# Two gated layers behind an attention: a Silu gate, sums off TensorE, products in pieces, new step tables

## The chip, the cores and the metric

The kernel runs on one core of a Trainium2 chip. The metric is the device time of one execution in microseconds; less is better. The core's engines are named as in the profile: PE is TensorE (PEld its weight loads), DVE is VectorE, ACT is ScalarE, POOL is GpSimd, SP is the engine whose queue issues the DMAs.

## The reference

```python
# q, k, v: (8, 8, 576, 64); phi: (8, 8, 576, 32)
a = exp(phi - max(phi, axis=2)); a = a / (sum(a, axis=2) + 1e-9)
k_m = einsum('bhsm,bhsd->bhmd', a, k)
v_m = einsum('bhsm,bhsd->bhmd', a, v)
scores = 1 / sqrt(64) * q @ k_m.T
attn = exp(scores - max(scores)); attn = attn / (sum(attn) + 1e-9)
x = (attn @ v_m) as (4608, 512)          # tokens x (heads * 64)
h = x @ w_in;  g = h / (1 + exp(-1.702 * h));  x = g @ w_out      # first layer, d_ff 2048
h = x @ w_in2; g = h / (1 + exp(-h));          out = g @ w_out2   # second layer
```

## The kernel before

The whole program is one list of instructions per engine, written in an order that tables set; each engine takes its own in order. Every product is made in three passes over high and low halves of the operands (PASSES), so that a tile of the first layer's hidden values is six matmuls.

**First stage: attention and the first layer's first product.** The outer loop runs over 128 steps, 16 for each of the 8 batches: two halves `i` of a batch's tokens (288 each) by eight blocks `f` of 256 hidden columns. A step has three slots, `x = 3 * s + u`. Slots u = 0 and 1 call `first`, which makes one h tile (128 hidden columns by 288 tokens, six matmuls into one of four banks of PSUM) and gates it; slot u = 2 stores the pair of gated tiles to DRAM (`store`). Before a slot's `first`, everything that the tables put on that slot is emitted. The gate was Tanh on ScalarE (L390) and a combining step on VectorE (L391) that reads the bank once more; the result is twice g, and the factor 0.25 in `b_copy` and `b_add` (with the product's own structure) takes it back.

The first product's weights depend on the batch: w' = v_m @ w_in, made in four blocks of 512 columns, `wp_mm` (TensorE, L340), `wp_hi` and `wp_lo` (high and low half of a slab). So each batch needs, ahead of its first h tile: loads of phi, k, v, q; the maximum of phi (`phi_max` and three small steps); `phi_sub`, `phi_exp`; `kv_mm`, 9 chunks of eight products of key and value with the exponentials, 144 matmuls (L207); the sums of the exponentials; `kv_norm`, `kv_t`, `kv_e`; six transposes of q (`q_t`, `q_e`); and for each half `scores`, `soft1`, `soft_sub`, `soft_exp`, `soft2`, `soft_mul`, `soft3`, `soft_hi`, `soft_lo`. Batches 2 to 7 take the sums on GpSimd (`phi_sum`, five adds) and one small product (`es_mm`); batches 0 and 1 take them on TensorE, by matmuls of two columns inside `kv_mm` (L214, 144 in each batch).

`TIMES` gives for batches 1, 2, 3 and all later ones the slot of every step, relative to the batch's first slot 48b; `on` says which of two engines does some of them. `FIRST` is the order of everything ahead of slot 0 (batch 0, and the weight tiles 0 to 3 that make column block 0 of w_in), and `BEGIN` places the rest of w_in's 16 tiles and batch 0's last steps. A weight tile is loaded (`w1_load`, L59, 0.5 MB), then converted by two steps on ScalarE (L78, L88), one on VectorE (L96) and one on GpSimd (L98). `WO` places the same for the first layer's w_out.

All DMAs are issued by SP in program order. Four banks of PSUM serve all of the attention's small products (`psa`), four the h tiles.

**Later stages.** From 382 us on the first layer's second product (`middle`, L787), then the second layer (L571, L686). They read what the first stage stored.

## Time and profile before

| | |
|---|---|
| median of 3 runs | 1441.04 us (1438.67 to 1444.81) |
| profiled execution | 1444.52 us, its span 1442.5 us |
| busy share of the span | PE 96%, PEld 92%, DVE 72%, ACT 55%, POOL 22% |
| mean granted TensorE clock | 0.989 |
| DMA | 277 MB, mean 192 GB/s |

Times in the rows are microseconds from the start of the span. Busy time is the time in which an engine had an instruction running; matmuls overlap each other, so that a busy TensorE is not one at its peak. "Idle before" names how long the engine stood still ahead of an instruction, and what released it.

### The profile page before, as it was taken

What the parts mean: (1) busy time and instruction counts of PE and PEld (TensorE: products, weight loads), DVE (VectorE), ACT (ScalarE), POOL (GpSimd) and SP (SyncE); (2) the same over time, 40 slices, a digit from 0 to 9 for tenths busy, and PEclk for the clock granted to TensorE, in tenths of its full rate; (3) what the DMA queues carried; (4) which work ended last, traced back from release to release, by engine and by line L of the source; (5) the groups of instructions that cost most, each with busy time, mean ns of one, the idle gap of its engine ahead of it and who ended that gap; (6) DMA issues with size and microseconds to landing.
All of it is one profiled execution on the core that took longest, in us unless ns stands there. A gap on an engine that the chain in (4) does not pass through costs nothing.

```text
span 1442.5 us, 26633 instructions
## 1 busy us (share of the span) xinstructions
PE 1385.5 (96%) x10288; PEld 1324.9 (92%) x10288; DVE 1044.5 (72%) x1490; ACT 794.4 (55%) x1395; POOL 323.9 (22%) x225
## 2 busy tenths in 40 slices
...
GB/s 343 191 172 262 262 286 267 267 270 186 328 282 165 263 92 225 214 135 236 87 122 191 199 174 196 215 154 218 167 194 186 208 89 132 202 49 187 125 106 33
DMA packets 217727, 276.99 MB, mean 192 GB/s; under 512 B 50689, under 2 KB 198145, under 8 KB 217601
## 3 DMA queue, kind: packets, MB, share of 16 engines
...
q8 instruction: 80, 1.31, 0.4%
q14 instruction: 47, 0.38, 0.1%
...
## 4 chain that ended last, share of the span: by engine, by line
PE 87%; DMA 3%; ACT 2%; DVE 2%; issue 2%; SPq 0%; POOL 0%; DVEq 0%; ACTq 0%; POOLq 0%
PE p L686 24%; PE pb L787 24%; PE xb L571 14%; PE h L388 10%; PE y L571 10%; PE a L340 2%; DMA g1s<-g 1%; DMA w1t<-wq 1%; PE a L207 1%; PE a L253 1%; ACT g L390 1%; DMA rawe<-in_moe_w_out_dram 1%; PE a L276 1%; DVE g L391 1%; DMA phi<-in_phi_dram 0%
## 5 line engine op out<-in xcount | busy, mean ns | idle before, releaser
L787 PE MATMUL pb<-op,wq 128*128 128x384 f32 x2016 | 350.5, 335 | 1.3 <-ACT op L766 0.8
L787 PEld LDWEIGHTS pb<-op,wq 128*128 128x128 f32 x2016 | 349.7, 188 | 1.9 <-ACT op L766 1.1
L686 PE MATMUL p<-op,wq 128*128 128x384 f32 x2016 | 351.0, 335 | 0.0
L686 PEld LDWEIGHTS p<-op,wq 128*128 128x128 f32 x2016 | 349.6, 188 | 1.3 <-DVE op L462 1.3
L462 DVE TENSOR_TENSOR op<-rr,op 128x768 fp32r<-128x768 f32 x204 | 238.0, 1176 | 49.1 <-ACT op L671 26.6
L388 PEld LDWEIGHTS h<-attnT,slab 128*128 128x128 f32 x1536 | 213.8, 193 | 37.5 <-DVE g L391 14.5
L388 PE MATMUL h<-attnT,slab 128*128 128x288 f32 x1536 | 237.2, 307 | 9.2 <-DVE g L391 3.8
L571 PE MATMUL xb<-xq,wq 128*128 128x384 f32 x1152 | 216.8, 337 | 0.3 <-ACT e L620 0.2
L571 PEld LDWEIGHTS xb<-xq,wq 128*128 128x128 f32 x1152 | 201.4, 188 | 1.4 <-ACT e L620 0.5
L866 POOL TENSOR_TENSOR c<-c 128x512 int32<-128x512 int32 x32 | 49.7, 1553 | 614.4 <-DVE c L864 526.8
L462 DVE TENSOR_TENSOR op<-r,op 128x768 fp32r<-128x768 f32 x132 | 144.9, 1106 | 37.8 <-ACT op L766 25.1
L391 DVE SCALAR_TENSOR_TENSOR g<-g,h 128x288 f32<-128x288 f32 x256 | 108.6, 447 | 84.3 <-ACT g L390 83.8
L571 PE MATMUL y<-xq,wq 128*128 128x384 f32 x864 | 166.2, 336 | 0.2 <-ACT e L631 0.2
L571 PEld LDWEIGHTS y<-xq,wq 128*128 128x128 f32 x864 | 151.6, 188 | 0.5 <-ACT e L631 0.5
L390 ACT ACTIVATE g<-h 128x288 f32<-128x288 f32 x256 | 100.3, 415 | 92.1 <-PE h L388 77.3
L671 ACT CAST op<-rr 128x768 fp32r<-128x768 f32 x108 | 89.7, 838 | 98.5 <-PE p L686 63.1
L580 ACT ACTIVATE gq<-e 128x384 f32<-128x384 f32 x144 | 75.6, 525 | 102.7 <-DVE e L459 101.6
L766 ACT CAST op<-rr 128x768 fp32r<-128x768 f32 x96 | 79.9, 835 | 68.0 <-PE pb L787 39.9
L459 DVE TENSOR_TENSOR e<-e,y 128x384 f32<-128x384 f32 x96 | 52.8, 553 | 60.8 <-PE y L571 53.7
L766 ACT CAST op<-r 128x768 fp32r<-128x768 f32 x72 | 60.2, 836 | 50.7 <-PE pb L787 43.6
L459 POOL TENSOR_TENSOR r<-r 128x768 f32<-128x768 f32 x10 | 22.6, 2284 | 273.5 <-DMA r<-gs 154.8
L459 DVE TENSOR_TENSOR e<-e,xb 128x384 f32<-128x384 f32 x48 | 26.5, 552 | 78.6 <-ACT c L859 34.4
...
## 6 DMA issues: line engine op xcount, KB each, us to landing
g1s<-g SPq DMA_DIRECT2D x128, 288.0 KB, 4.4
gs<-gq SPq DMA_DIRECT2D x192, 192.0 KB, 1.9
...
```

The source lines that it names most:

```text
L388: nc.tensor.matmul(out=h, lhsT=w[:, wi, g, f0:f0 + 128], rhs=x[:, xi, g * HS:(g + 1) * HS], start=(g == 0 and n == 0), stop=(g == 1 and n ...
L390: nc.scalar.activation(out=t[:, u], in_=h, func=ACTF.Tanh, scale=0.851)
L391: nc.vector.scalar_tensor_tensor(out=t[:, u], in0=t[:, u], scalar=1.0, in1=h, op0=ALU.add, op1=ALU.mult)
L459: eng.tensor_tensor(out=out, in0=a, in1=b, op=ALU.add)
L462: eng.tensor_tensor(out=out, in0=a, in1=b, op=ALU.subtract)
L571: nc.tensor.matmul(out=out, lhsT=w[:, s, wi, f0:f0 + 128], rhs=x[:, s, xi], start=(start and s == 0 and k == 0), stop=(s == 1 and k == 2), ...
L580: nc.scalar.activation(out=t, in_=h, func=ACTF.Silu, scale=2.0)
L671: nc.scalar.copy(out=t[:, :, 0], in_=s)
L686: nc.tensor.matmul(out=out[:, d], lhsT=w[:, u, wi, d * 128:(d + 1) * 128], rhs=t[:, u, gi], start=(start and p == 0 and u == 0 and k == 0) ...
L766: nc.scalar.copy(out=t[:, :, 0], in_=s)
L787: nc.tensor.matmul(out=out[:, d, :HB], lhsT=w[:, u, wi, d * 128:(d + 1) * 128], rhs=t[:, u, gi], start=(start and p == 0 and u == 0 and n ...
L866: nc.gpsimd.tensor_tensor(out=i, in0=i, in1=low, op=ALU.add)
```

## The change

The first layer's gate becomes one Silu on ScalarE with scale 1.702, which gives 1.702 g; `HALF` = 0.5 / 1.702 takes the place of 0.25 behind the second product. The sums of batches 0 and 1 are taken like those of the others, batch 0's adds on VectorE. The copies `q_e`, `soft_hi` and `wp_hi` can be on either ScalarE or VectorE, by new entries of `on` and of the tables. All of `TIMES`, `FIRST`, `BEGIN` and `WO` is new: among it the slots of the products' pieces (`k`), of the Exp steps (`exp`, and the fourth entry in each tuple of `s`) and the order of the first loads.

```diff
@@ -32,6 +32,7 @@
     NP = NF // 2
     NG = 2 * HS // 32
     scale = 1.0 / float(D) ** 0.5
+    HALF = 0.5 / 1.702
...
@@ -184,14 +185,14 @@
         t = st["phi", b][:, :, c0:c1]
         nc.scalar.activation(out=t, in_=t, func=ACTF.Exp)
 
-    def phi_sum(b):
+    def phi_sum(b, eng):
         e = st["es", b] = att.tile([128, 2, 4, M], F32, tag="kvb", name="es", bufs=2)
         t = st["phi", b]
         c = t.rearrange("p j c m -> p c j m")
         for n in range(3):
-            nc.gpsimd.tensor_tensor(out=e, in0=e if n else c[:, 0:2], in1=c[:, 2 * n + 2:2 * n + 4], op=ALU.add)
-        nc.gpsimd.tensor_tensor(out=e[:, 0], in0=e[:, 0], in1=e[:, 1], op=ALU.add)
-        nc.gpsimd.tensor_tensor(out=e[:, 0], in0=e[:, 0], in1=t[:, :, 8], op=ALU.add)
+            eng.tensor_tensor(out=e, in0=e if n else c[:, 0:2], in1=c[:, 2 * n + 2:2 * n + 4], op=ALU.add)
+        eng.tensor_tensor(out=e[:, 0], in0=e[:, 0], in1=e[:, 1], op=ALU.add)
+        eng.tensor_tensor(out=e[:, 0], in0=e[:, 0], in1=t[:, :, 8], op=ALU.add)
...
@@ -207,13 +208,6 @@
                     nc.tensor.matmul(out=a[s][32 * j:32 * j + 32, 0:2 * D], lhsT=e[p, j, c, :],
                                      rhs=t[p, :, j, (c - c0) * D:(c - c0 + 1) * D],
                                      start=(c == 0), stop=(c == C9 - 1), skip_group_check=True)
-            if b < 2:
-                for j in range(4):
-                    for s in range(2):
-                        p = slice(64 * s, 64 * s + 64)
-                        nc.tensor.matmul(out=a[s][32 * j:32 * j + 32, 2 * D:2 * D + 2], lhsT=e[p, j, c, :],
-                                         rhs=ones[p].to_broadcast([64, 2]), start=False, stop=(c == C9 - 1),
-                                         skip_group_check=True)
 
     def es_mm(b):
         es = st.pop(("es", b))[:, 0].rearrange("p j m -> p (j m)")
...
-    def q_e(b, n):
+    def q_e(b, n, copy):
         if n % 3 == 0:
             st["qT", b, n // 3] = att.tile([128, C9, 128], F32, tag="qT", name="qT", bufs=2)
         t = st["qT", b, n // 3]
         a = st.pop(("qp", b, n))[:, 0:384].rearrange("p (k x) -> p k x", k=3)
-        nc.scalar.copy(out=t[:, 3 * (n % 3):3 * (n % 3) + 3], in_=a)
+        copy(out=t[:, 3 * (n % 3):3 * (n % 3) + 3], in_=a)
...
-    def soft_hi(b, hf):
+    def soft_hi(b, hf, copy):
         t = attnT[b, hf] = moe.tile([128, 2, 2 * HS], F32R, tag="attnT", name="attnT", bufs=2)
-        nc.scalar.copy(out=tokens(t[:, 0]), in_=blocks(st["at", b, hf]))
+        copy(out=tokens(t[:, 0]), in_=blocks(st["at", b, hf]))
...
-    def wp_hi(b, c):
+    def wp_hi(b, c, copy):
         t = slab[b, c] = slabs.tile([128, 2, 2, 512], F32R, tag="slab", name="slab", bufs=4)
         for s, a in enumerate(st["wp", b, c]):
-            nc.scalar.copy(out=t[:, 0, s], in_=a)
+            copy(out=t[:, 0, s], in_=a)
...
@@ -387,8 +381,7 @@
             for n, (wi, xi) in enumerate(PASSES):
                 nc.tensor.matmul(out=h, lhsT=w[:, wi, g, f0:f0 + 128], rhs=x[:, xi, g * HS:(g + 1) * HS],
                                  start=(g == 0 and n == 0), stop=(g == 1 and n == 2))
-        nc.scalar.activation(out=t[:, u], in_=h, func=ACTF.Tanh, scale=0.851)
-        nc.vector.scalar_tensor_tensor(out=t[:, u], in0=t[:, u], scalar=1.0, in1=h, op0=ALU.add, op1=ALU.mult)
+        nc.scalar.activation(out=t[:, u], in_=h, func=ACTF.Silu, scale=1.702)
...
     def b_copy(bank):
         t = eb_tile()
-        nc.scalar.activation(out=t, in_=bank[:, :, :HB], func=ACTF.Copy, scale=0.25)
+        nc.scalar.activation(out=t, in_=bank[:, :, :HB], func=ACTF.Copy, scale=HALF)
         return t
 
     def b_add(t, bank):
-        nc.vector.scalar_tensor_tensor(out=t, in0=bank[:, :, :HB], scalar=0.25, in1=t, op0=ALU.mult, op1=ALU.add)
+        nc.vector.scalar_tensor_tensor(out=t, in0=bank[:, :, :HB], scalar=HALF, in1=t, op0=ALU.mult, op1=ALU.add)
 
...
             put(z + t["exp"][g], phi_exp, b, g)
         for n in range(4):
             put(z + t["k"][n], kv_mm, b, n)
-        if b > 1:
-            put(z + t["es"][0], phi_sum, b)
-            put(z + t["es"][1], es_mm, b)
+        put(z + t["es"][0], phi_sum, b, nc.gpsimd)
+        put(z + t["es"][1], es_mm, b)
         for x, fn in zip(t["kvt"], (kv_norm, kv_t, kv_e)):
             put(z + x, fn, b)
         for n in range(6):
             put(z + t["q"][n], q_t, b, n)
-            put(z + t["qe"][n], q_e, b, n)
+            put(z + t["qe"][n], q_e, b, n, COPY[t["on"][3][n]])
         steps = scores, soft1, soft_sub, soft_exp, soft2, soft_mul, soft3, soft_hi, soft_lo
         for hf in range(2):
             on = iter(t["on"][hf])
             for x, fn in zip(t["s"][hf], steps):
-                put(z + x, fn, b, hf, *((ENG[next(on)],) if fn in (soft_sub, soft_mul, soft_lo) else ()))
+                by = ENG if fn in (soft_sub, soft_mul, soft_lo) else COPY if fn == soft_hi else None
+                put(z + x, fn, b, hf, *((by[next(on)],) if by else ()))
         for c in range(4):
-            plan_wprime(b, c, z, t["wp"][c])
-
-    def plan_wprime(b, c, z, x):
-        for y, fn in zip(x, (wp_mm, wp_hi, wp_lo)):
-            put(z + y, fn, b, c)
+            for x, fn, a in zip(t["wp"][c], (wp_mm, wp_hi, wp_lo), ((), (COPY[t["on"][2][c]],), ())):
+                put(z + x, fn, b, c, *a)
 
     ENG = nc.vector, nc.gpsimd
+    COPY = nc.scalar.copy, nc.vector.tensor_copy
+    BY = dict(ps=ENG, ss=ENG, sm=ENG, lo=ENG, hi=COPY, qe=COPY, wh=COPY)
     TIMES = {
-        1: dict(ql=(-36, -28), max=(-39, -39, -39, -38, -38), t=(-36, -36, -34), sub=(-33, -32), exp=(-27, -26),
-                k=(-22, -18, -18, -18), es=(-20, -7), kvt=(-18, -16, -15), q=(-26, -25, -22, -20, -18, -15),
-                qe=(-22, -21, -21, -18, -17, -15),
-                s=((-13, -12, -12, -10, -9, -8, -7, -6, -6), (-6, -6, 0, 1, 1, 5, 10, 15, 22)),
-                wp=((-11, -9, -9), (-4, -2, -2), (-1, 0, 4), (3, 5, 7)), on=((1, 1, 1), (1, 0, 1))),
-        2: dict(load=(-79, -68, -57), ql=(-48, -34), max=(-74, -70, -70, -68, -67), t=(-62, -58, -56),
-                sub=(-56, -53), exp=(-54, -48), k=(-39, -39, -39, -39), es=(-44, -36), kvt=(-36, -34, -32),
-                q=(-38, -37, -35, -30, -30, -27), qe=(-37, -36, -33, -28, -27, -27),
-                s=((-25, -24, -21, -20, -19, -16, -16, -7, -3), (-8, -6, -3, 0, 2, 2, 11, 18, 20)),
-                wp=((-18, -15, -12), (-11, -9, -9), (-6, -3, 1), (6, 7, 9)), on=((1, 0, 1), (1, 1, 1))),
-        3: dict(load=(-103, -91, -82), ql=(-77, -52), max=(-97, -97, -97, -90, -89), t=(-87, -86, -83),
-                sub=(-79, -76), exp=(-74, -71), k=(-55, -55, -55, -55), es=(-56, -54), kvt=(-53, -43, -42),
-                q=(-45, -39, -38, -35, -34, -31), qe=(-40, -39, -33, -34, -34, -31),
-                s=((-30, -30, -25, -23, -20, -19, -13, -13, -9), (-14, -12, -10, -5, 1, 8, 13, 14, 16)),
-                wp=((-20, -19, -19), (-10, -4, -1), (1, 3, 3), (4, 5, 7)), on=((1, 0, 1), (0, 0, 1))),
-        4: dict(load=(-102, -96, -72), ql=(-72, -49), max=(-96, -94, -93, -89, -89), t=(-86, -82, -79),
-                sub=(-79, -79), exp=(-74, -72), k=(-55, -55, -55, -55), es=(-61, -52), kvt=(-49, -40, -38),
-                q=(-42, -41, -40, -39, -34, -32), qe=(-41, -40, -39, -34, -33, -31),
-                s=((-28, -27, -22, -20, -18, -15, -14, -12, -8), (-15, -12, -11, -7, -4, -2, 2, 9, 15)),
-                wp=((-16, -16, -16), (-13, -12, -12), (-3, 3, 3), (3, 3, 5)), on=((1, 1, 1), (1, 1, 1))),
+        1: dict(ql=(-39, -32), max=(-43, -39, -39, -38, -38), t=(-37, -36, -34), sub=(-31, -28), exp=(-28, -28),
+                k=(-23, -19, -19, -19), es=(-28, -18), kvt=(-18, -16, -15), q=(-25, -25, -22, -18, -17, -15),
+                qe=(-22, -21, -21, -18, -15, -14),
+                s=((-13, -12, -12, -10, -9, -7, -7, -5, -4), (-4, -2, 1, 2, 2, 4, 7, 9, 20)),
+                wp=((-11, -9, -9), (-1, 0, 1), (-2, -1, 3), (2, 4, 6)),
+                on=((1, 1, 0, 1), (1, 1, 0, 0), (0, 1, 0, 0), (0, 1, 0, 1, 1, 1))),
+        2: dict(load=(-74, -63, -60), ql=(-46, -37), max=(-68, -66, -66, -64, -63), t=(-58, -58, -56),
+                sub=(-56, -51), exp=(-45, -46), k=(-39, -39, -39, -39), es=(-38, -36), kvt=(-35, -34, -31),
+                q=(-37, -36, -36, -30, -29, -29), qe=(-36, -34, -34, -30, -27, -27),
+                s=((-26, -24, -22, -22, -17, -15, -15, -12, -8), (-8, -5, -3, -1, 2, 2, 3, 16, 20)),
+                wp=((-17, -17, -15), (-11, -9, -9), (-11, -7, 0), (5, 5, 9)),
+                on=((1, 1, 1, 1), (0, 0, 1, 0), (1, 1, 0, 0), (0, 1, 0, 0, 0, 1))),
+        3: dict(load=(-105, -92, -81), ql=(-83, -53), max=(-97, -97, -97, -94, -90), t=(-87, -85, -82),
+                sub=(-76, -82), exp=(-70, -70), k=(-56, -56, -55, -55), es=(-60, -54), kvt=(-52, -44, -44),
+                q=(-46, -40, -39, -37, -34, -31), qe=(-40, -38, -32, -34, -33, -31),
+                s=((-31, -31, -31, -25, -19, -19, -15, -15, -12), (-22, -10, -7, 3, 10, 15, 18, 20, 21)),
+                wp=((-20, -20, -19), (-12, -4, 2), (2, 3, 6), (5, 9, 10)),
+                on=((1, 1, 0, 0), (0, 1, 1, 1), (0, 0, 1, 1), (1, 0, 1, 0, 1, 1))),
+        4: dict(load=(-103, -98, -70), ql=(-82, -54), max=(-95, -94, -93, -91, -89), t=(-86, -82, -79),
+                sub=(-76, -74), exp=(-73, -73), k=(-56, -55, -55, -52), es=(-59, -52), kvt=(-52, -44, -40),
+                q=(-42, -41, -40, -37, -34, -32), qe=(-42, -41, -37, -35, -34, -32),
+                s=((-29, -28, -24, -24, -22, -20, -12, -7, -4), (-15, -12, -11, -7, -4, 1, 5, 8, 18)),
+                wp=((-20, -18, -14), (-13, -12, -12), (-1, 2, 3), (3, 3, 5)),
+                on=((0, 1, 1, 0), (0, 1, 0, 0), (1, 1, 1, 0), (1, 0, 1, 1, 1, 0))),
     }
...
-        fns = dict(pm=phi_max, t=phi_max_t, r=phi_max_r, b=phi_max_b, sub=phi_sub, exp=phi_exp, kv=kv_mm, lphi=load_phi,
...
         for n, (f, *x) in enumerate(FIRST):
-            if f in ("ss", "sm", "lo"):
-                x[-1] = ENG[x[-1]]
+            if f in BY:
+                x[-1] = BY[f][x[-1]]
...
     FIRST = [
-        ('lphi', 0), ('pm', 0, 0), ('lq', 0, 0), ('lkv', 0, 0), ('lkv', 0, 1), ('pm', 0, 1), ('lw', 3), ('lw', 0),
-        ('lq', 0, 1), ('lkv', 1, 1), ('pm', 0, 2), ('pm', 0, 3), ('pm', 0, 4), ('lw', 1), ('lw', 6), ('lw', 2),
-        ('t', 0), ('lw', 4), ('lkv', 1, 0), ('lw', 7), ('r', 0), ('b', 0), ('sub', 0, 0), ('sub', 0, 1),
-        ('exp', 0, 0), ('exp', 0, 1), ('lw', 5), ('kv', 0, 0), ('kv', 0, 1), ('kv', 0, 2), ('w0', 0), ('kv', 0, 3),
-        ('nrm', 0), ('qt', 0, 0), ('qt', 0, 1), ('qe', 0, 0), ('kt', 0), ('qt', 0, 2), ('qe', 0, 1), ('ke', 0),
-        ('qt', 0, 3), ('w1', 0), ('qe', 0, 2), ('qt', 0, 4), ('qe', 0, 3), ('qe', 0, 4), ('qt', 0, 5), ('lw', 8),
-        ('qe', 0, 5), ('sc', 0, 0), ('w0', 1), ('s1', 0, 0), ('w0', 3), ('ss', 0, 0, 0), ('w0', 2), ('w1', 3),
-        ('lphi', 1), ('w1', 1), ('w1', 2), ('se', 0, 0), ('wp', 0, 0), ('wh', 0, 0), ('s2', 0, 0), ('sm', 0, 0, 0),
-        ('sc', 0, 1), ('s3', 0, 0), ('hi', 0, 0), ('lo', 0, 0, 1), ('s1', 0, 1), ('wl', 0, 0), ('ss', 0, 1, 1),
-        ('se', 0, 1), ('s2', 0, 1), ('sm', 0, 1, 1),
+        ('lphi', 0), ('pm', 0, 0), ('lq', 0, 0), ('lw', 0), ('lkv', 0, 0), ('pm', 0, 1), ('lw', 1), ('lkv', 0, 1),
+        ('pm', 0, 2), ('pm', 0, 3), ('lq', 0, 1), ('lw', 2), ('pm', 0, 4), ('lw', 3), ('lw', 4), ('t', 0), ('lw', 6),
+        ('r', 0), ('lw', 7), ('b', 0), ('sub', 0, 1), ('lkv', 1, 0), ('lw', 5), ('exp', 0, 1), ('sub', 0, 0),
+        ('qt', 0, 0), ('lkv', 1, 1), ('w0', 0), ('exp', 0, 0), ('kv', 0, 0), ('qt', 0, 1), ('w1', 0), ('kv', 0, 1),
+        ('ps', 0, 0), ('kv', 0, 2), ('kv', 0, 3), ('w0', 1), ('qe', 0, 0, 0), ('w0', 2), ('es', 0), ('nrm', 0),
+        ('qt', 0, 3), ('qt', 0, 4), ('qe', 0, 3, 1), ('qe', 0, 4, 0), ('qt', 0, 5), ('w0', 3), ('kt', 0), ('w1', 1),
+        ('qe', 0, 1, 0), ('w1', 2), ('qe', 0, 5, 0), ('qt', 0, 2), ('qe', 0, 2, 1), ('ke', 0), ('w1', 3),
+        ('sc', 0, 0), ('lw', 8), ('lphi', 1), ('s1', 0, 0), ('ss', 0, 0, 1), ('se', 0, 0), ('s2', 0, 0),
+        ('sm', 0, 0, 0), ('s3', 0, 0), ('sc', 0, 1), ('hi', 0, 0, 0), ('wp', 0, 0), ('s1', 0, 1), ('lo', 0, 0, 0),
+        ('wh', 0, 0, 0), ('ss', 0, 1, 1), ('se', 0, 1), ('s2', 0, 1), ('sm', 0, 1, 1), ('wl', 0, 0),
     ]
     BEGIN = [
...
+        (15, ('w1', 8)), (5, ('lw', 12)), (13, ('w0', 12)), (5, ('w0', 5)), (20, ('lw', 15)), (16, ('lw', 14)),
+        (11, ('wp', 0, 1)), (0, ('w0', 7)), (9, ('w1', 6)), (36, ('wl', 0, 3)), (0, ('lw', 10)),
+        (33, ('wh', 0, 3, 0)), (26, ('w0', 15)), (4, ('lw', 11)), (8, ('w1', 5)), (21, ('w0', 13)), (12, ('w1', 10)),
+        (7, ('w0', 6)), (3, ('w1', 7)), (28, ('w1', 15)), (12, ('w0', 9)), (22, ('w1', 12)), (11, ('lw', 13)),
+        (3, ('lo', 0, 1, 0)), (16, ('w1', 9)), (11, ('wh', 0, 1, 0)), (11, ('wl', 0, 1)), (21, ('wp', 0, 2)),
+        (0, ('w0', 8)), (32, ('wp', 0, 3)), (2, ('hi', 0, 1, 0)), (30, ('w1', 14)), (3, ('w0', 4)), (0, ('lw', 9)),
+        (24, ('wl', 0, 2)), (21, ('wh', 0, 2, 0)), (7, ('w0', 10)), (25, ('w0', 14)), (13, ('w0', 11)),
+        (23, ('w1', 13)), (4, ('w1', 4)), (0, ('s3', 0, 1)), (16, ('w1', 11)),
...
-    WO = dict(conv=((6, 17, 19, 22), (9, 24, 26, 29), (25, 35, 38, 39), (30, 41, 42, 45)),
-              sum=((45, 47, 59), (59, 62, 70), (62, 67, 68), (54, 55, 65), (48, 58, 60, 62), (47, 67, 68, 71), (78, 78, 81, 82)))
+    WO = dict(conv=((7, 15, 16, 17), (11, 24, 26, 31), (22, 32, 39, 39), (28, 38, 39, 40)),
+              sum=((43, 46, 55), (50, 59, 63), (66, 68, 73), (58, 62, 72), (46, 55, 55, 59), (48, 67, 67, 71), (71, 78, 78, 85)))
```

## Rows read from the trace of the kernel before

**Rows 1.** Busy time by stretch: time, busy (instructions) of each engine, granted clock, DMA

```profile
0.00:100.00 100.00, 68.06 (x1033) 50.58 (x1039) 57.17 (x113) 47.88 (x95) 30.32 (x28) 0.86 0.68 232
100.00:340.00 240.00, 225.92 (x2915) 190.51 (x2904) 180.55 (x406) 163.71 (x367) 127.77 (x112) 0.99 0.80 263
340.00:388.00 48.00, 43.13 (x326) 38.44 (x325) 29.34 (x62) 27.13 (x62) 17.78 (x14) 1.00 0.78 270
388.00:1442.50 1054.50, 1048.41 (x6023) 1045.35 (x6023) 777.43 (x911) 555.70 (x874) 148.00 (x72) 1.00 0.52 168
```

**Rows 2.** Timeline of TensorE around three stalls: start, length, instructions, idle before them

```profile
67.87 1.84 PE L388 MATMUL h<-attnT,slab 128*128 128x288 f32 x12
...
82.08 0.59 PE L253 MATMUL a<-ident,q 128*128 128x128 f32 x2 [5.51 <-issue]
82.32 3.23 PE L388 MATMUL h<-attnT,slab 128*128 128x288 f32 x12
85.48 1.79 PE L340 MATMUL a<-w,kvT 64*32 64x512 f32 x16
...
91.44 1.09 PE L340 MATMUL a<-w,kvT 64*32 64x512 f32 x16
...
263.28 2.03 PE L207 MATMUL a<-kv,phi 64*32 64x128 f32 x128
267.38 0.45 PE L207 MATMUL a<-kv,phi 64*32 64x128 f32 x16 [2.07 <-issue]
...
310.16 0.41 PE L207 MATMUL a<-kv,phi 64*32 64x128 f32 x4 [2.31 <-issue]
```

**Rows 3.** The page: engines; instruction queue (packets, MB, share); one group of the second layer

```profile
PE 1385.5 (96%) x10288; PEld 1324.9 (92%) x10288; DVE 1044.5 (72%) x1490; ACT 794.4 (55%) x1395; POOL 323.9 (22%) x225
...
q8 instruction: 80, 1.31, 0.4%
...
L580 ACT ACTIVATE gq<-e 128x384 f32<-128x384 f32 x144 | 75.6, 525 | 102.7 <-DVE e L459 101.6
```

**Rows 4.** Busy time by stretch, up to two stalls and behind one, columns as above

```profile
0.00:76.65 76.65, 50.54 (x853) 38.20 (x854) 44.76 (x84) 38.59 (x76) 26.72 (x25) 0.87 0.77 269
82.10:85.50 3.40, 3.40 (x18) 3.12 (x17) 0.46 (x1) 0.78 (x2) 0.00 (x0) 0.50 0.02 5
0.00:265.60 265.60, 224.37 (x3135) 181.13 (x3135) 187.77 (x400) 161.01 (x347) 117.62 (x106) 0.95 0.78 259
```

**Rows 5.** Groups of ScalarE and VectorE, 0 to 380 us: busy, mean ns | idle before

```profile
L390 ACT ACTIVATE g<-h 128x288 f32<-128x288 f32 x252 | 98.8, 415 | 87.3 <-PE h L388 77.3 <-DMA g1s<-g 7.5 <-DMA w1t<-wq 1.8
...
L297 ACT ACTIVATE nat<-nat 128x576 f32<-128x576 f32 x16 | 11.0, 688 | 5.9 <-POOL nat L293 5.9
...
L185 ACT ACT_TABLE_LOAD x1 | 1.3, 1283 | 4.9 <-DMA phi<-in_phi_dram 4.9
...
L391 DVE SCALAR_TENSOR_TENSOR g<-g,h 128x288 f32<-128x288 f32 x252 | 107.0, 447 | 80.2 <-ACT g L390 79.7
```

**Rows 6.** Timeline of ScalarE around its second table load

```profile
386.11 1.57 ACT L766 CAST op<-rr 128x768 fp32r<-128x768 f32 x2
387.70 1.28 ACT L1075 ACT_TABLE_LOAD   x1
388.99 0.20 ACT L1075 ACTIVATE spare<-ones 128x1 f32<-128x1 f32 x1
```

**Rows 7.** Timeline of ScalarE and TensorE, batch 0 up to slot 12

```profile
16.06 0.66 ACT L78 ACTIVATE w<-rawe 128x512 f32<-128x512 f32 x1 [5.39 <-DMA rawe<-in_moe_w_in_dram]
...
30.62 2.32 PE L340 MATMUL a<-w,kvT 64*32 64x512 f32 x8 [5.18 <-POOL w L98]
...
37.86 5.44 PE L388 MATMUL h<-attnT,slab 128*128 128x288 f32 x23 [1.19 <-POOL attnT L332]
...
46.16 4.77 PE L388 MATMUL h<-attnT,slab 128*128 128x288 f32 x23 [1.40 <-POOL attnT L332]
...
53.40 1.06 PE L340 MATMUL a<-w,kvT 64*32 64x512 f32 x8 [0.38 <-POOL w L98]
...
56.00 1.78 PE L388 MATMUL h<-attnT,slab 128*128 128x288 f32 x10 [0.34 <-DVE slab L351]
```

5 lines of the change are left out of this document (3 added, 2 removed), and 8 rows, old and new, of the table BEGIN.

## The prediction

> **What bounds the kernel now.** I read busy time by stretch first, then TensorE's own timeline wherever it stood still, then the groups by line. The stretches [rows 1] say where anything can be won: after 388 us TensorE is idle for 6 us in 1054, and the diff leaves that part alone but for one constant in b_copy and b_add, so the whole question lies in the first 388 us. Up to 100 us it is idle for 32 of 100 us, and its mean granted clock is 0.86. From 100 to 340 us it is idle for 14 of 240. No other engine is full there (VectorE 181, ScalarE 164, GpSimd 128 of 240), so the stage is TensorE's plus stalls.
>
> The stalls with a name are in [rows 2]. The longest have no releaser at all, only "issue": 5.51 us right behind batch 1's key/value products, 2.07 in batch 6's, 2.31 in batch 7's. I read these as TensorE running out of instructions. Its 10288 matmuls and as many weight loads came in 80 instruction packets [rows 3], 128.6 pairs each. Up to the first two stalls 853 and 3135 matmuls are recorded [rows 4], 2282 apart or 17.8 packets (some records are missing). So I place each at a packet border, after a burst of small matmuls: 128 pairs went by in 2.03 us before the second [rows 2], where a tile of six h matmuls takes 0.92 us (12 in 1.84). Behind the long stall, in which TensorE did nothing, the granted clock is 0.50 from 82.1 to 85.5 us [rows 4], the lower level of 1.2 GHz, and 12 h matmuls take 3.23 us [rows 2].
>
> **The change part by part.**
>
> *Two-column matmuls of batches 0 and 1.* They are 144 of the 288 matmuls in a batch's burst. Without them batch 1's burst is 144 pairs, little over one packet, and the new table cuts it in 48 at slot 25 and 96 at slot 29 with three h tiles between; the loads of batch 2's keys move from slots 28 and 39 to 33 and 36, away from it. Gain: the stall, 5.51; the slow clock behind it, 3.23 - 1.84 = 1.39 for the h tiles, 1.79 - 1.09 = 0.7 for 16 products of w' (85.48 against 91.44); and the 144 pairs, at 2.03/128 = 16 ns each at most 2.3, at least 0, I take 1.5 because they interleave with wider ones. Together 9.1, bounds 2 (the stall stays, only the pairs go) and 10. What they cost instead: five adds per batch off the path (batch 0's on VectorE while TensorE still waits for k and v, batch 1's on GpSimd, which is idle 112 of 240 us) and four small matmuls, 0.1 us.
>
> *Key/value products in pieces.* Batches 4 to 7 get 48 pairs, an h tile, 64 pairs, two h tiles, 32 pairs. The packet that ran dry lasted 2.03 us and its successor came 2.07 us later, so a fetch took about 4.1 us. In the new order the first 112 pairs and three tiles, 130 pairs, last 112 x 16 ns + 3 x 0.92 = 4.6 us. That covers the fetch. Gain 2.07 + 2.31, plus a slow clock after the first like that above, about 1.4: 5.8 at most. But some 560 instructions fewer ahead shift every packet border, and batches 2 (one burst of 144) and 3 (80 and 64 with one tile between) could now hit one, for up to 2.1 us each. I take 4, bounds 0 and 5.8.
>
> *First loads and batch 0.* In the new order the second half of k and v ends 4.58 MB into the queue, where in the old one the first weight tile that was converted ended (4.59 MB, in at 16.06 us [rows 7]). So batch 0's products end near 17.5. Weight tiles 2 and 3, at the mean rate until then (0.286 MB/us), are in at about 20 and 21.7; with ScalarE, VectorE and GpSimd each taking its part of the conversion, I get w' of column block 0 started near 27, where it waited until 30.62 for GpSimd. Against that stands one thing that gets later: the low half of that block (wl) is now the last step of FIRST on VectorE, behind the other half's transposes, soft_lo and sums. The first tile's third matmul needs it, and I place it at 38.4, an estimate from walking each engine's order in FIRST; the old one went on at 37.86. Then the second half's attention is ready when the first four tiles are done, near 44.1 instead of 46.16, because soft_lo is on VectorE without waiting on GpSimd's queue, and block 1 of w' can start near 49 instead of 53.40, since VectorE has no gate steps between the shifts that GpSimd waits for. Slot 12 then starts near 52 instead of 56.00 [rows 7]. Batch 1's k and v now stand on SP's queue behind seven weight tiles; its first product is at slot 25, and 16 h tiles hide that. Gain 4, bounds -2 (the late low half and a weight that lands late each cost 3) and 8.
>
> *Gate as one Silu.* VectorE loses 256 steps of 447 ns, 114 us [rows 5], and takes back 28 copies of q, 7 of the attention's high halves and 34 of w', at L390's rate (415 ns for 288 elements) at most 0.83 us each, 57 us, and 13 of soft_lo and 8 more of soft_sub from GpSimd. VectorE, ScalarE and GpSimd all end with slack, and TensorE waits for none of them by their sum. Silu itself is no dearer than Tanh: 525 ns for 384 elements [rows 3] is 394 for 288. The h bank comes free one step sooner. I price the removed step at nothing directly, because four banks covered it.
>
> *Tables.* This is the cost. The whole first stage has one table load, ahead of the first Exp (L185); Tanh needed none [rows 5], Silu did (L1075) [rows 6]. With Silu between, every visit to Exp needs a load there and one back. Counting the Exp steps by slot, adjacent ones merged, I find 15 visits: slot 20 with both phi steps; 50, 74, 119, 167, 215 and 263 with three Exp steps; eight with one. So 30 more loads of 1.283 us, 38.5 us of ScalarE. If Silu's set held Exp as well they would fall away; no row shows it, and that is the lower bound, 0. In the trace the load stands flush: the step before it ends at 387.68, it runs from 387.70, the next starts at 388.99. A visit of one Exp blocks the gates for 2 x 1.28 + 0.69 = 3.25 us, and with the last gate before (0.42) and the first after (0.41) a bank is late by 4.1; four tiles last 3.7, and other work of TensorE between them 1.5 more (240 us held some 180 tiles of 0.92, the rest is 0.37 per tile). So a single visit is hidden, and would cost 0.4 without that cover. A triple visit, with two phi steps as long as the soft one, takes 4.6 us and is late by 5.4 against 5.2, or 3.7 uncovered: 0.2 to 1.7. Sum 1.2 to 14.5, slot 20 included. Visits come on top of w' copies queued behind, so I take 3.
>
> By the Trainium skill (ScalarE: Activation LUTs, What ACT_TABLE_LOAD costs) a switch costs 1283 ns of load and about 1380 ns of drain, 2.66 us together. The trace agrees on the load and shows no drain beside it; by the page, the triple visit would be 2.75 us longer, the sum of all visits near 33 us, and the kernel slower.
>
> *The other waits.* Of the 14 us idle from 100 to 340, 9.7 are short waits for VectorE, ScalarE and GpSimd. Fewer VectorE steps shorten some, new tables make others: 2 gained, between -3 and 6. The last 48 us (5 us idle, gates waiting for stores while the first layer's output is read back) keep the same transfers: 0. The new WO slots are hidden as they were by GpSimd's slack.
>
> Sum: 9 + 4 + 4 + 2 - 3 = 16 us.
>
> **Rivals.** *Packets still run dry* (chance 0.17): the borders move onto batches 2 and 3, and batch 1's second piece hits one while its neighbours load. For it: with the same burst batches 6 and 7 ran dry and 2 to 5 did not, so it is the border's place that decides. Against: shorter bursts. The gain of 13 falls to 3, and the time is 10 us above the forecast, 1435.
> *Table visits exposed* (0.11, ends slower): ScalarE waits in its order for an Exp whose input is late, gates behind it, and each visit shows both loads in full: 15 x 2.57 = 38.5. The sum without visits is 19, so the time is 19.5 above now, 1460. It decides from (19 + 7)/15 = 1.7 us per visit. Against it: the four banks and the 0.37 us per tile. The page's drain, named above, would bring 1441 - 19 + 33 = 1455; the chance of this rival is small because the one switch amid work shows no gap.
> *No switches needed, or more waits gone* (0.10): visits 0 and waits 6, 1441 - 9 - 8 - 6 - 6 (batch 0, pieces and waits at their bounds) = 1412.
> *Batch 0's gain is lost* (0.08): the low half of w' is later than I place it; +6, 1431.
>
> **How the numbers follow.** The profiled execution took 1444.5 us, its span 1442.5, the median is 1441.04; I take the 16 from the median: 1425. Its own range, by the terms' nearer bounds, is 1416 to 1433, chance 0.54. To hold 8 in 10 the range goes up to the packets' rival and the start of no change, 1443, and down to 1409. A measurement of this kernel can tell about 0.5%, 7.2 us. Faster 0.76 (0.54 + 0.10 + 0.08 and a quarter of the packets' rival), same 0.13 (the rest of that), slower 0.11.
>
> **What the after profile would show.** Right: no "issue" wait over 1 us inside the key/value products, granted clock 1.0 from 75 us on, wp of block 3 (slot 32) near 72 us instead of 85.48, 32 table loads in all, ScalarE 160 to 170 us busy from 100 to 340 and VectorE near 150, the end of the first stage some 16 us earlier. Wrong: TensorE waits for the gate by more than 1 us at Exp visits; h waits for the slab's low half beyond 40 us; "issue" waits at other bursts.

## The result: 1427.68 us, 1.0% faster

The median falls from 1441.65 us (1438.67 to 1444.81, 4 runs) to 1427.68 us (1424.47 to 1428.38, 4 runs), a ratio of 0.9898 with a 95% interval of 0.9872 to 0.9925. The forecast was 1425. The profiled execution took 1428.18 us, its span 1426.4; against before's 1444.52 that is 16.3 us less, where the sum said 16. So the profiles, which the points below compare, differ by some 2 us more than the medians.

The page of after, its engines and instruction queue (to be held against [rows 3]):

```profile
PE 1381.7 (97%) x10008; PEld 1318.3 (92%) x10008; DVE 1011.7 (71%) x1326; ACT 800.6 (56%) x1356; POOL 303.4 (21%) x212
...
q8 instruction: 78, 1.28, 0.4%
```

Its busy time by stretch, columns as in [rows 1]; the first stage's end is taken 14 us earlier:

```profile
0.00:100.00 100.00, 73.72 (x980) 53.52 (x981) 62.56 (x116) 62.96 (x114) 39.31 (x40) 0.95 0.82 277
100.00:340.00 240.00, 232.19 (x2823) 192.92 (x2823) 165.26 (x293) 167.92 (x336) 117.20 (x99) 1.00 0.79 257
340.00:374.00 34.00, 29.36 (x200) 28.08 (x199) 8.49 (x10) 15.87 (x38) 2.44 (x2) 1.00 0.95 310
374.00:1426.40 1052.40, 1046.46 (x6012) 1043.83 (x6010) 775.38 (x909) 553.90 (x870) 144.44 (x72) 1.00 0.52 168
```

Behind the first stage nothing moved: from the next stage's first matmul to the end it is 1061.0 us against 1060.7. Up to 100 us TensorE is busy for 73.7 instead of 68.1 us, and from 100 to 340 it is idle for 7.8 instead of 14.1.

TensorE's timeline (to be held against [rows 2] and [rows 7]): batch 0 up to slot 12, slot 32, the longest of the waits that are left (two of the four for the gate), and the next stage's first matmul:

```profile
37.27 5.20 PE L382 MATMUL h<-attnT,slab 128*128 128x288 f32 x23 [2.97 <-DVE slab L345]
42.98 3.33 PE L382 MATMUL h<-attnT,slab 128*128 128x288 f32 x23 [0.52 <-DVE attnT L326]
...
48.34 1.06 PE L334 MATMUL a<-w,kvT 64*32 64x512 f32 x8 [0.70 <-POOL w L99]
...
50.80 1.79 PE L382 MATMUL h<-attnT,slab 128*128 128x288 f32 x10 [0.19 <-DVE slab L345]
...
70.68 1.09 PE L334 MATMUL a<-w,kvT 64*32 64x512 f32 x16
...
91.32 1.68 PE L334 MATMUL a<-w,kvT 64*32 64x512 f32 x16 [1.51 <-DVE slab L345]
...
96.32 2.20 PE L208 MATMUL a<-kv,phi 64*32 64x128 f32 x138
99.98 0.42 PE L208 MATMUL a<-kv,phi 64*32 64x128 f32 x6 [1.47 <-issue]
...
119.98 2.65 PE L382 MATMUL h<-attnT,slab 128*128 128x288 f32 x18 [0.96 <-ACT g L384]
...
241.68 1.86 PE L382 MATMUL h<-attnT,slab 128*128 128x288 f32 x12 [1.10 <-ACT g L384]
...
365.44 4.40 PE L780 MATMUL pb<-op,wq 128*128 128x384 f32 x24
```

Three sums can be read off. Slot 12 starts at 50.80 instead of 56.00: 5.2 us. From there to the product of batch 0's last column block (slot 32) it is 19.88 us instead of 29.48 (85.48 - 56.00): 9.6. From there to the next stage's first matmul, 294.76 instead of 296.35 (that matmul began at 381.83): 1.6. Together 16.4.

Batches 0 and 1 go through their products without a stall; batch 2, whose burst of 144 is whole, now has one. At four of the six triple table visits TensorE waits for the gate, 0.95 to 1.10 us each. ScalarE's timeline at the visit of slot 74, the one in front of that wait:

```profile
114.65 0.41 ACT L384 ACTIVATE g<-h 128x288 f32<-128x288 f32 x1 [0.34 <-PE h L382]
115.08 1.28 ACT L291 ACT_TABLE_LOAD   x1
116.37 0.69 ACT L291 ACTIVATE nat<-nat 128x576 f32<-128x576 f32 x1
116.97 1.24 ACT L186 ACTIVATE phi<-phi 128x640 f32<-128x640 f32 x2
118.22 1.28 ACT L384 ACT_TABLE_LOAD   x1
119.52 1.32 ACT L384 ACTIVATE g<-h 128x288 f32<-128x288 f32 x4
```

From the last gate's end to the next gate's start it is 4.46 us, and the loads stand flush between their neighbours. The Trainium skill (ScalarE: Activation LUTs, What ACT_TABLE_LOAD costs) gives 1283 ns of load, which these rows show, and about 1380 ns of drain beside it, which they don't.

### The profile page after: what moved, and what is told of

Read it like the earlier page. It is cut to its first block, busy times and chain, and to the rows that moved or that the text cites. A ratio compares the mean times of both kernels' runs of the same rounds, so it can differ in the third digit from the quotient of the medians.

```text
span 1426.4 us, 25738 instructions
## 1 busy us (share of the span) xinstructions
PE 1381.7 (97%) x10008; PEld 1318.3 (92%) x10008; DVE 1011.7 (71%) x1326; ACT 800.6 (56%) x1356; POOL 303.4 (21%) x212
## 4 chain that ended last, share of the span: by engine, by line
PE 87%; DVE 3%; ACT 3%; DMA 2%; issue 2%; SPq 0%; POOL 0%; DVEq 0%; ACTq 0%; POOLq 0%
PE pb L780 24%; PE p L679 21%; PE xb L564 14%; PE h L382 11%; PE y L564 10%; PE a L334 2%; PE a L208 1%; DVE op L455 1%; PE a L247 1%; DMA g1s<-g 1%; PE a L270 1%; ACT g L384 1%; ACT L384 0%; DMA rr<-gs 0%; DMA rawe<-in_moe_w_out_dram 0%
## 5 line engine op out<-in xcount | busy, mean ns | idle before, releaser
L382 PEld LDWEIGHTS h<-attnT,slab 128*128 128x128 f32 x1536 | 210.4, 190 | 51.7 <-ACT g L384 21.3
L859 POOL TENSOR_TENSOR c<-c 128x512 int32<-128x512 int32 x32 | 46.6, 1457 | 619.2 <-DVE c L857 528.0
L759 ACT CAST op<-r 128x768 fp32r<-128x768 f32 x72 | 60.2, 836 | 52.6 <-PE pb L780 43.7
L664 ACT CAST op<-r 128x768 fp32r<-128x768 f32 x60 | 50.2, 837 | 56.5 <-PE p L679 45.1
```

The lines of the kernel that those rows point to most:

```text
L382: nc.tensor.matmul(out=h, lhsT=w[:, wi, g, f0:f0 + 128], rhs=x[:, xi, g * HS:(g + 1) * HS], start=(g == 0 and n == 0), stop=(g == 1 and n ...
L664: nc.scalar.copy(out=t[:, :, 0], in_=s)
L759: nc.scalar.copy(out=t[:, :, 0], in_=s)
L859: nc.gpsimd.tensor_tensor(out=i, in0=i, in1=low, op=ALU.add)
```

## The experiments

Each is timed against the kernel before on the same chip; ratios are to that kernel, with 95% intervals.

### Where do the stalls without a releaser come from?

The theory is that TensorE's instructions arrive in packets and that it runs dry where a packet lies whole in a burst of small matmuls. If so, useless instructions far ahead move the stalls.

**64 useless pairs in the kernel before.** At slot 6 TensorE does 32 tiny products (64 matmuls and weight loads in the trace) into a free bank; nothing else changes.

```diff
+    def idle_pairs(n):
+        h = ps_h.tile([128, 512], F32, tag="h", name="h")
+        for k in range(n // 2):
+            nc.tensor.matmul(out=h[0:32, 0:2], lhsT=ident[0:64, 0:32], rhs=ident[0:64, 0:2], start=True, stop=True)
...
-        (13, ('w1', 9)), (32, ('wp', 0, 3)), (15, ('w0', 12)), (21, ('wh', 0, 2)), (28, ('lw', 15)), (8, ('w1', 5)),
+        (6, ('idle', 64)), (13, ('w1', 9)), (32, ('wp', 0, 3)), (15, ('w0', 12)), (21, ('wh', 0, 2)), (28, ('lw', 15)), (8, ('w1', 5)),
```

> The kernel before plus 64 useless two-column matmul pairs on TensorE at slot 6, where it waits for batch 0's second attention half anyway. They compute nothing that is used. Theory of the prediction: every packet border falls 64 pairs earlier in the work behind; in batches 6 and 7 no packet lies whole in a burst any more, so the stalls of 2.07 and 2.31 us and the slow clock behind the first vanish, that of batch 1 (a burst of 192 pairs) stays. 4 to 6 us faster, ratio 0.996 to 0.997. Rival (the stalls come from the loads that run beside these bursts, or from the bursts themselves): stalls stay, the time is 0 to 1 us longer, ratio 1.000.

Measured 1434.03 us (1429.55 to 1435.42), ratio 0.9942 (0.9926 to 0.9958): added work makes the kernel 8 us faster (its profiled execution was its fastest, and shows more). That is above the 4 to 6 us expected, because batch 1's stall, which was to stay, nearly went too. Its TensorE timeline shows the added pairs, batch 1's stall cut to 0.39, and batch 7's burst whole (batch 6's is too; batch 0's stall, ahead of the added pairs, stays at 3.12; one wait of 0.81 on issue is new, behind batch 3's burst):

```profile
43.25 2.25 PE L960 MATMUL h<-ident 64*32 64x2 f32 x64 [0.72 <-DVE g L391]
...
75.47 0.34 PE L207 MATMUL a<-kv,phi 64*32 64x128 f32 x7 [0.39 <-issue]
...
293.58 2.25 PE L207 MATMUL a<-kv,phi 64*32 64x128 f32 x144
```

**126 useless pairs**, nearly one packet: the borders should fall back to where they were. The diff is to the kernel with 64.

```diff
-        (6, ('idle', 64)), (13, ('w1', 9)), (32, ('wp', 0, 3)), (15, ('w0', 12)), (21, ('wh', 0, 2)), (28, ('lw', 15)), (8, ('w1', 5)),
+        (6, ('idle', 126)), (13, ('w1', 9)), (32, ('wp', 0, 3)), (15, ('w0', 12)), (21, ('wh', 0, 2)), (28, ('lw', 15)), (8, ('w1', 5)),
```

> The kernel before plus 126 useless two-column pairs at slot 6, in place of the 64 of the earlier run: almost one whole packet (126.75 pairs by the gaps between the stalls). Theory (packet borders): every border lies again within a pair of where it was in the work, so the stalls behind batch 1 and in batches 6 and 7 are back, 1.5 to 2.5 us each in 6 and 7, 2 to 6 in batch 1; the time is that of the kernel before or up to 2 us more, ratio 0.999 to 1.002. Rival (the 64 pairs helped by keeping TensorE busy, by another bank order or by something else early on): faster as with 64 pairs, ratio 0.994.

Measured 1446.45 us (1442.02 to 1448.72), ratio 1.0037 (1.0022 to 1.0051). The stalls are back, 4.08 us behind batch 1's burst, and in batches 6 and 7 at nearly the matmuls where they were:

```profile
83.24 3.01 PE L388 MATMUL h<-attnT,slab 128*128 128x288 f32 x11 [4.08 <-issue]
...
263.71 2.15 PE L207 MATMUL a<-kv,phi 64*32 64x128 f32 x130
266.89 0.45 PE L207 MATMUL a<-kv,phi 64*32 64x128 f32 x14 [1.03 <-issue]
...
308.00 0.38 PE L207 MATMUL a<-kv,phi 64*32 64x128 f32 x2 [2.11 <-issue]
```

That tells packets from any rule of how long TensorE had been idle or busy: the two kernels differ in 62 tiny pairs at 43 us, and the stalls at 266 and 308 us come and go with them. Before has a fourth such stall, which the prediction did not read, inside batch 0's burst:

```profile
18.16 0.21 PE L214 MATMUL a<-ones,phi 64*32 64x2 f32 x5 [2.89 <-issue]
```

The four stalls of before lie 632, 2282 and 507 recorded pairs apart, that is 5, 18 and 4 packets of 126.4 to 126.8 pairs. Counting on with 126.75, four packets of before lie in a burst whole or but for two pairs: in batches 0, 1, 6 and 7, which are the four that stalled.

**Batches 0 and 1 without their two-column matmuls**, the first part alone, in the kernel before.

```diff
-            if b < 2:
-                for j in range(4):
-                    for s in range(2):
...
-        if b > 1:
-            put(z + t["es"][0], phi_sum, b)
-            put(z + t["es"][1], es_mm, b)
+        put(z + t["es"][0], phi_sum, b)
+        put(z + t["es"][1], es_mm, b)
...
-                k=(-22, -18, -18, -18), es=(-20, -7), kvt=(-18, -16, -15), q=(-26, -25, -22, -20, -18, -15),
+                k=(-22, -18, -18, -18), es=(-20, -18), kvt=(-18, -16, -15), q=(-26, -25, -22, -20, -18, -15),
...
-        ('exp', 0, 0), ('exp', 0, 1), ('lw', 5), ('kv', 0, 0), ('kv', 0, 1), ('kv', 0, 2), ('w0', 0), ('kv', 0, 3),
+        ('exp', 0, 0), ('exp', 0, 1), ('ps', 0), ('lw', 5), ('kv', 0, 0), ('kv', 0, 1), ('kv', 0, 2), ('w0', 0), ('kv', 0, 3), ('es', 0),
```

> The kernel before with one part alone: the two-column matmuls of batches 0 and 1 are gone, their sums taken as those of the other batches. Theory of the prediction (TensorE runs out of instructions where a whole packet of 127 pairs lies in a burst of small matmuls): the 5.5 us stall behind batch 1's products is gone, and since 280 pairs fewer shift the packet borders, those of batches 6 and 7 go as well and stalls of 1.5 to 2.3 us each come in batches 2, 4 and 5, whose bursts now hold a whole packet. Time about 1434, ratio 0.993 to 0.996. Rival (the two-column matmuls are slow in themselves, stalls belong to batches 6 and 7): stalls in batches 6 and 7 stay, none in 2, 4, 5; ratio about 0.993. Rival (the gain is VectorE's relief by the gate): ratio above 0.998.

Measured 1439.5 us (1434.09 to 1446.02), ratio 0.9979 (0.9964 to 0.9993), some 3 us. The stalls of batches 0 and 1 are gone. Slot 12 comes 3.3 us earlier than in before under the old loads, and TensorE is 9.6 us ahead of before when it reaches batch 2's maximum of phi (79.25 against 88.82). Most of that is lost again. Batch 2's burst now stalls; by the count a packet lies whole in it. From 100 to 340 us the waits on issue are 8.0 us against 4.4. And this kernel adds a wait of its own, because batch 1's adds stand on GpSimd behind a weight conversion:

```profile
52.71 1.79 PE L381 MATMUL h<-attnT,slab 128*128 128x288 f32 x10 [0.34 <-DVE slab L344]
...
74.22 0.39 PE L215 MATMUL a<-ones,es 64*128 64x2 f32 x4 [2.96 <-POOL es L194]
...
100.21 2.20 PE L207 MATMUL a<-kv,phi 64*32 64x128 f32 x139
106.53 0.41 PE L207 MATMUL a<-kv,phi 64*32 64x128 f32 x5 [4.12 <-issue]
```

**The two-column matmuls put back into after**, all else as after.

```diff
+            if b < 2:
+                for j in range(4):
+                    for s in range(2):
...
-        put(z + t["es"][0], phi_sum, b, nc.gpsimd)
-        put(z + t["es"][1], es_mm, b)
+        if b > 1:
+            put(z + t["es"][0], phi_sum, b, nc.gpsimd)
+            put(z + t["es"][1], es_mm, b)
```

> The kernel after with one part undone: the two-column matmuls of batches 0 and 1 are back in the bursts, the five adds and the small product of each batch gone. Theory (packets that run dry, longest where k and v of the next batch are being loaded): batch 1's burst at slot 29 is 192 pairs again, one packet lies in it almost whole (121 of 127), so a stall of 2 to 5 us comes back there and the pairs cost 1.5: 3 to 8 us more than the kernel after, ratio to the kernel before 0.992 to 0.996. Rival (their price is the pairs alone): 1 to 2 us more, 0.991. Rival (the new loads order has already moved the loads away, nothing comes back): no issue wait over 0.5 us in batch 1.

Measured 1428.21 us (1425.81 to 1433.41), ratio 0.9922 (0.9901 to 0.9944): by medians not to be told from after, by ratios 3.5 us slower, with intervals that overlap. Slot 12 comes at 52.97 instead of 50.80, slot 32 at 75.72 instead of 70.68, with issue waits of 2.12 us in batch 0 and 1.32 behind batch 1; but the 2.6 us of issue waits that after has in batches 2, 6 and 7 are gone, and the next stage begins at 365.20 against 365.44. So the 5.0 us that the matmuls cost up to slot 32 come back behind it: half of that in borders, 0.5 in a shorter wait for a slab, the rest in places that were not traced.

**After with batches 3 to 7 in one burst.**

```diff
-                sub=(-76, -82), exp=(-70, -70), k=(-56, -56, -55, -55), es=(-60, -54), kvt=(-52, -44, -44),
+                sub=(-76, -82), exp=(-70, -70), k=(-55, -55, -55, -55), es=(-60, -54), kvt=(-52, -44, -44),
...
-                sub=(-76, -74), exp=(-73, -73), k=(-56, -55, -55, -52), es=(-59, -52), kvt=(-52, -44, -40),
+                sub=(-76, -74), exp=(-73, -73), k=(-55, -55, -55, -55), es=(-59, -52), kvt=(-52, -44, -40),
```

> The kernel after with one part undone: the products of batches 3 to 7 in one burst of 144 pairs each. Theory: whole packets (127 pairs) then lie in the bursts of batches 4 and 5, which stall 0.3 to 2.3 us each, batch 2 keeps its 1.47, batch 6 (115 pairs) up to 1.6; 2 to 5 us more than the kernel after, ratio 0.992 to 0.994. Rival (pieces do nothing where they stand): the same as the kernel after, 0.990.

Measured 1427.68 us (1424.79 to 1431.45), ratio 0.9918 (0.9896 to 0.9941). The issue waits grow, with one in batch 3 longer than any of after:

```profile
132.01 1.19 PE L208 MATMUL a<-kv,phi 64*32 64x128 f32 x47 [3.24 <-issue]
```

That is not as the count had it. It put a whole packet into the bursts of batches 4 and 5 and none into batch 3's. But batch 3, with 97 pairs of its burst ahead of the border, has the longest wait, batch 4 waits 0.49 us and batch 5 not at all. All in all the waits on issue from 90 to 340 us are 6.7 us against 2.6; the next stage begins 1.7 us later. By medians the pieces can't be told from nothing, by ratios they bring 2.9 us (0.0020 of 1441), within both intervals.

### What do the table visits cost?

**After with one Tanh in place of the Silu**, in the same place and with the same operands. It leaves out the gate's product with h. Exp and Tanh together need no switch: 2 loads in all.

```diff
-        nc.scalar.activation(out=t[:, u], in_=h, func=ACTF.Silu, scale=1.702)
+        nc.scalar.activation(out=t[:, u], in_=h, func=ACTF.Tanh, scale=0.851)
```

> The kernel after with the gate as one Tanh in place of one Silu: the gate's product with h is left out, every instruction keeps its size, and Exp and Tanh share a table set, so only the table loads of the 15 visits go. Theory of the prediction (a visit costs TensorE about 1 us only where three Exp steps meet): 1 table load instead of 32, the four waits of about 1 us for the gate vanish, 3 to 5 us less than the kernel after, ratio to the kernel before 0.986 to 0.988. Rival (the loads are exposed and hold back much of the gain): 15 us less or more, ratio 0.980 or lower. Rival (loads free): no change against the kernel after, 0.990.

Measured 1416.26 us (1412.99 to 1419.44), ratio 0.9819 (0.9798 to 0.9839): 11.4 us under after by medians, 8.7 at the next stage's first matmul (356.78). Its busy time by stretch:

```profile
100.00:340.00 240.00, 238.33 (x2875) 200.74 (x2874) 166.35 (x295) 142.55 (x324) 120.45 (x100) 0.99 0.79 264
```

TensorE is idle for 1.7 us instead of 7.8. The view of TensorE's waits from 85 to 340 us, first of after (engine and line that waited, for whom; us in all, times, longest):

```profile
PE h L382 <- ACT g L384: 4.1, 4, 1.1
PE a L334 <- DVE slab L345: 2.8, 2, 1.5
PE a L208 <- issue: 2.6, 3, 1.5
...
PE a L270 <- DVE qT L254: 0.5, 1, 0.5
```

And the same view of the kernel with Tanh:

```profile
PE a L334 <- DVE slab L345: 2.1, 2, 1.5
PE a L208 <- issue: 2.0, 1, 2.0
...
PE h L382 <- ACT g L384: 0.5, 1, 0.5
```

So 3.6 us of the visits' price are waits for the gate itself, and 1.2 are waits for copies made on VectorE (slab 0.7, qT 0.5). The longest wait for a slab, 1.5 us ahead of batch 1's last w' product, stands in both kernels and is no price of a visit. More shows at slot 38, a single visit with two copies of w' queued behind its Exp on ScalarE. TensorE's timeline a few slots behind it, two rows of after, then the same two of the kernel with Tanh:

```profile
81.71 1.27 PE L270 MATMUL a<-qT,kvT 64*32 64x160 f32 x32
...
84.09 1.92 PE L334 MATMUL a<-w,kvT 64*32 64x512 f32 x16
...
80.81 0.72 PE L270 MATMUL a<-qT,kvT 64*32 64x160 f32 x32
...
82.46 1.23 PE L334 MATMUL a<-w,kvT 64*32 64x512 f32 x16
```

From the start of each row to the next h tile it is 1.39 and 1.86 us in after, 0.65 and 1.16 with Tanh. The views count no wait of TensorE there, but the two steps are drawn out by 1.4 us together. Slot 20's visit, with copies of w' behind it as well, costs 0.8 us (by slot 32 the Tanh kernel is 0.9 ahead, at slot 12 it was 0.1). The comparison is not quite clean: the Tanh kernel's own wait on issue in batch 2 is 2.00 us instead of 1.47, and from 98.2 to 105.4 us its granted clock is 0.76, which after does not have.

**After with Silu in place of Exp at the eight single visits.** It leaves out the softmax of those eight halves; 16 loads remain.

```diff
-        nc.scalar.activation(out=n, in_=n, func=ACTF.Exp, scale=scale)
+        alone = (b, hf) in ((1, 0), (2, 1), (3, 1), (4, 1), (5, 1), (6, 1), (7, 0), (7, 1))
+        nc.scalar.activation(out=n, in_=n, func=ACTF.Silu if alone else ACTF.Exp, scale=scale)
```

> The kernel after with the Exp of the eight visits that stand alone replaced by a Silu of the same size (the softmax of these halves is left out), so that their 16 table loads go and the triple visits stay. Theory as the prediction had it (a single visit is hidden, the triples pay): 0 to 2 us less than the kernel after, ratio 0.988 to 0.990, four waits for the gate of about 1 us stay. Rival (every visit pays about alike, 11 us over 15): 5 to 7 us less, ratio 0.985 to 0.987.

Measured 1422.06 us (1421.18 to 1426.42), ratio 0.9882 (0.9864 to 0.9901): 5.6 us under after by medians, but 2.3 by ratios, within both intervals. The next stage begins at 359.47, 6.0 us earlier. The four gate waits stay as they were (4.1 us in all), so they belong to the triple visits. The two rows of slot 38 are 0.72 and 1.23 us again, as with Tanh: that single visit costs 1.4 us, though no gate waits there. The waits for a slab fall only from 2.8 to 2.6. What the other seven cost is less sure. Of the 6.0 us about 1 was there at slot 12, ahead of the first visit that the edit touches, and 2.4 are issue waits, which fell from 2.6 to 0.2; the reordered kernel below has just 0.3 of them with all its visits, so they are not the visits' price.

**The Silu alone in the kernel before**, with its old tables and its copies on ScalarE.

```diff
-        nc.scalar.activation(out=t[:, u], in_=h, func=ACTF.Tanh, scale=0.851)
-        nc.vector.scalar_tensor_tensor(out=t[:, u], in0=t[:, u], scalar=1.0, in1=h, op0=ALU.add, op1=ALU.mult)
+        nc.scalar.activation(out=t[:, u], in_=h, func=ACTF.Silu, scale=1.702)
```

> The kernel before with one part alone: the gate as one Silu, under the old tables, where the Exp steps meet less often (about 28 visits, 56 more table loads, 72 us of ScalarE). Theory of the prediction (VectorE's relief is worth 0 to 4 us on TensorE's path, a visit 0 to 0.4 us): between 3 us faster and 8 us slower, ratio 0.998 to 1.006. Rival (the relief of VectorE is the source of the gain): 8 us faster or more, ratio under 0.995. Rival (loads exposed): 28 x 2.57 = 72 us slower, ratio 1.05.

Measured 1482.83 us (1480.12 to 1487.85), ratio 1.0284 (1.0263 to 1.0306), 41 us slower. The old tables scatter the Exp steps: 58 loads, 28 visits between gates, some of them with only two gates between. ScalarE's timeline there:

```profile
136.71 1.28 ACT L186 ACT_TABLE_LOAD   x1
138.01 0.74 ACT L186 ACTIVATE phi<-phi 128x640 f32<-128x640 f32 x1
138.76 1.28 ACT L391 ACT_TABLE_LOAD   x1
140.06 0.71 ACT L391 ACTIVATE g<-h 128x288 f32<-128x288 f32 x2
140.79 1.28 ACT L186 ACT_TABLE_LOAD   x1
```

And the first line of the view of TensorE's waits from 100 to 340 us, columns as above:

```profile
PE h L389 <- ACT g L391: 26.7, 13, 3.7
```

TensorE waits for the gate 13 times, 2.1 us each on average. That two gates between two visits don't refill four banks fits this, but it is argued from the timeline. At 1.5 us a visit (41 us over 28, with whatever VectorE's relief gives back already in it) this comes near the 1.7 from which the rival with exposed visits decides. Under the new tables the Silu is affordable; which part of them does it, the merged Exp steps or the copies moved off ScalarE, was not tried apart.

### What do the first loads bring?

**After with the loads of FIRST in their old sequence**, the computing steps as in after.

```diff
-        ('lphi', 0), ('pm', 0, 0), ('lq', 0, 0), ('lw', 0), ('lkv', 0, 0), ('pm', 0, 1), ('lw', 1), ('lkv', 0, 1),
-        ('pm', 0, 2), ('pm', 0, 3), ('lq', 0, 1), ('lw', 2), ('pm', 0, 4), ('lw', 3), ('lw', 4), ('t', 0), ('lw', 6),
...
+        ('lphi', 0), ('pm', 0, 0), ('lq', 0, 0), ('lkv', 0, 0), ('lkv', 0, 1), ('pm', 0, 1), ('lw', 3), ('lw', 0),
+        ('pm', 0, 2), ('pm', 0, 3), ('lq', 0, 1), ('lkv', 1, 1), ('pm', 0, 4), ('lw', 1), ('lw', 6), ('t', 0), ('lw', 2),
...
```

> The kernel after with one part undone: the loads in FIRST follow one another as in the kernel before, in the places of the new order; all other steps stay. Theory (the new loads bring the weights of block 0 in time, worth part of the 5.2 us by which slot 12 is earlier): the conversions of block 0 wait for weights 1 and 2 and the first tiles come 1 to 4 us later, ratio 0.991 to 0.993. Rival (the order of the steps gives it all, the loads none): slot 12 stays at 50 us, ratio 0.990.

Measured 1430.54 us (1426.45 to 1432.38), ratio 0.9927 (0.9912 to 0.9942), and slot 12 at 54.96 instead of 50.80. ScalarE's timeline shows the conversion of weight tile 0 waiting. An Exp of phi stands behind it there, and TensorE's timeline shows its first key/value products waiting for that Exp (2.35 us in after):

```profile
15.55 0.66 ACT L79 ACTIVATE w<-rawe 128x512 f32<-128x512 f32 x1 [5.82 <-DMA rawe<-in_moe_w_in_dram]
...
17.45 1.54 PE L208 MATMUL a<-kv,phi 64*32 64x128 f32 x48 [8.28 <-ACT phi L186]
```

So under the new steps the old loads lose 4.2 us at slot 12. That does not make the loads worth 4.2 of the 5.2: it is the new steps that put a weight's conversion ahead of the Exp. Without the two-column matmuls slot 12 came 3.3 us earlier under the old loads and steps, and putting them back into after made it 2.2 later. The three parts overlap, and no run has the new loads under the old steps.

**After with the end of FIRST reordered**: the second half's scores and soft steps between the first half's, w' and its high half earlier, the low half still last.

```diff
-        ('sc', 0, 0), ('lw', 8), ('lphi', 1), ('s1', 0, 0), ('ss', 0, 0, 1), ('se', 0, 0), ('s2', 0, 0),
-        ('sm', 0, 0, 0), ('s3', 0, 0), ('sc', 0, 1), ('hi', 0, 0, 0), ('wp', 0, 0), ('s1', 0, 1), ('lo', 0, 0, 0),
-        ('wh', 0, 0, 0), ('ss', 0, 1, 1), ('se', 0, 1), ('s2', 0, 1), ('sm', 0, 1, 1), ('wl', 0, 0),
+        ('sc', 0, 0), ('lw', 8), ('lphi', 1), ('s1', 0, 0), ('sc', 0, 1), ('wp', 0, 0), ('ss', 0, 0, 1), ('s1', 0, 1),
+        ('ss', 0, 1, 1), ('se', 0, 0), ('wh', 0, 0, 0), ('s2', 0, 0), ('se', 0, 1), ('sm', 0, 0, 0), ('s3', 0, 0),
+        ('s2', 0, 1), ('sm', 0, 1, 1), ('hi', 0, 0, 0), ('lo', 0, 0, 0), ('wl', 0, 0),
```

> The kernel after with the last steps of FIRST in another order: the second half's soft1 and soft_sub stand right behind the first half's soft1, and the high and low half of w' block 0 ahead of where they were. Theory of the prediction (the late low half holds the first tiles, the second half's attention the next ones): the first tiles go on at 34 to 35 us instead of 37.27, the fifth at 38 to 40 instead of 42.98, 2 to 4 us less than the kernel after, ratio 0.987 to 0.988, if the weights of block 1 are converted as much earlier. Rival (those conversions set slot 12): the tiles start earlier, slot 12 stays at 50 us, no gain, 0.990.

Measured 1422.13 us (1418.78 to 1422.84), ratio 0.987 (0.9851 to 0.989). Its slowest execution is faster than the fastest of after, though the intervals of the ratios overlap; no version that computes the whole reference had a lower median. TensorE's timeline:

```profile
32.65 4.92 PE L382 MATMUL h<-attnT,slab 128*128 128x288 f32 x23 [0.65 <-DVE attnT L326]
...
39.60 3.33 PE L382 MATMUL h<-attnT,slab 128*128 128x288 f32 x23 [0.87 <-DVE attnT L326]
...
47.39 1.79 PE L382 MATMUL h<-attnT,slab 128*128 128x288 f32 x10 [0.19 <-DVE slab L345]
```

The first tiles go on 4.6 us earlier than in after (37.27), slot 12 is reached 3.4 us earlier (50.80), the next stage 5.7 us (at 359.71). Part of that is again where borders fall: its waits on issue from 85 to 340 us are 0.3 us against 2.6.

**On top of that, batch 2's products in pieces.**

```diff
-                sub=(-56, -51), exp=(-45, -46), k=(-39, -39, -39, -39), es=(-38, -36), kvt=(-35, -34, -31),
+                sub=(-56, -51), exp=(-45, -46), k=(-41, -39, -38, -36), es=(-38, -36), kvt=(-35, -34, -31),
```

> As the run before, and batch 2's products in four pieces at slots 55, 57, 58 and 60. Theory: no packet with more than 109 of 127 pairs in bursts is left, batch 2's stall of 1.47 us goes down to 0.5 or less; 1 to 2 us less than the run before. Rival: stalls move to other batches, no change.

Measured 1423.24 us (1420.76 to 1424.4), ratio 0.9881 (0.9862 to 0.9901): no gain over the reordering alone, whose issue wait in batch 2 was down to 0.32 us already.

**The reordering with 64 useless pairs.** The diff is to the reordered kernel; `idle_pairs` is that of the first experiment.

```diff
-        (15, ('w1', 8)), (5, ('lw', 12)), (13, ('w0', 12)), (5, ('w0', 5)), (20, ('lw', 15)), (16, ('lw', 14)),
+        (6, ('idle', 64)), (15, ('w1', 8)), (5, ('lw', 12)), (13, ('w0', 12)), (5, ('w0', 5)), (20, ('lw', 15)), (16, ('lw', 14)),
```

> The kernel after with the earlier second half and 64 useless pairs at slot 6. By the packet borders no burst holds more than 106 of 127 pairs (104 behind batch 1), so the issue waits of the run with the earlier half alone (0.32 us in batch 2 in its profile) should go below 0.3 us each. Theory: the same as that run or up to 2 us less, ratio 0.985 to 0.987. Rival (the pairs stand in the way of the first tiles): 1 us more.

Measured 1423.67 us (1420.0 to 1424.81), ratio 0.9877 (0.986 to 0.9894): nothing left to win by shifting borders.

## Why the prediction was right, term by term

*Where the time is.* Right: nothing behind the first stage, the gain in the stalls up to 100 us and in the waits up to 340. The reading of the stalls without a releaser as packet borders is shown by the two shifted kernels. It missed batch 0's stall of 2.89 us, longer than two of the three that it named, and 128.6 pairs a packet was a little high: at 126.75 the 2282 between its first two stalls are 18.0 packets, where it made 17.8 of them.

*Two-column matmuls, 9 us: right in the trace, too narrow as a cause.* Slot 12 to slot 32 lost 9.6 us, the stall of batch 1 and its slow clock (0.50) are gone, and wp of block 3 runs at 70.68 where "near 72" was said. But the term put this down to the removed matmuls. Removed alone they bring 9.6 us by batch 2's maximum of phi and 3 us at the end, because other bursts stall instead; put back into after they cost between nothing and 3.5 us. The gain at the end is one of where all instructions together put the borders, and the sums' removal is one of several ways to move them.

*Pieces, 4 us: too large.* After's issue waits are smaller by 4.1 us than in one burst, but the next stage comes only 1.7 us sooner and the medians agree. Batch 2 did hit a border, as the term warned, for 1.47 of the 2.1 us allowed.

*First loads, 4 us: 5.2.* The placed times held within 2 us: products end at 17.61 (17.5 said), tiles go on at 37.27 behind the late low half (38.4), the fifth tile begins at 42.98 (44.1), block 1 of w' at 46.24, its second half at 48.34 (near 49), slot 12 at 50.80 (near 52). But what the gain comes from was wrong in part. Batch 0's stall went with its two-column matmuls, which alone moved slot 12 by 3.3 us; the loads and steps were not separated from that. The late low half was the real cost that was seen: the reordered end of FIRST removes it and gains more.

*Table visits, 3 us: the mis-sized term.* The Tanh kernel shows 8.7 (first matmul) to 11.4 us (medians), inside the bounds of 1.2 to 14.5 but near the upper one. The loads were counted right (32) and stand flush but for one gap of 0.66 us, and four triple visits showed 0.95 to 1.10 us of gate wait within the 0.2 to 1.7 that was worked out. The step that failed is that a single visit is hidden: it looked at the gate alone and put too little on "w' copies queued behind". At slot 38 a visit with two such copies behind it cost 1.4 us with no gate waiting, at slot 20 it was 0.8, and waits for other copies came to 1.2. With the 3.6 of the gate that is 7.0; where the rest of the 8.7 to 11.4 us goes stays open.

*Other waits, 2 us: too small.* They hid that error. That the sum came out within 3 us of the median is partly luck: two misses cancelled. From slot 32 to the next stage the Tanh kernel takes 287.00 us (356.78 - 69.78), 9.4 less than before, where pieces and other waits were given 6; with the visits in, after gains 1.6 there. Which waits went with VectorE's 256 steps the runs don't separate. ScalarE's 168 us from 100 to 340 is as forecast; VectorE's 165 is 15 over what was said, and as an engine's sum it still bounds nothing.

*The rivals.* Packets still run dry: in small (2.6 us), not at the 10 that it needs. Exposed visits: not in after; under the old tables the Silu comes near it, at 1.5 us a visit of the 2.57 that the rival gives. The extra 2.75 us that a drain would have put on a triple visit are not in its 4.46. Batch 0's gain was not lost. The granted clock was 1.00 from 75 to 340 us, as said, batch 2's short stall included.

*The signs.* Two of the three signs of being wrong came: TensorE waits for the gate by more than 1 us at two visits (1.08 and 1.10), and there are issue waits at other bursts. The sign of being right that allowed no issue wait over 1 us failed at batch 2's 1.47. The third, h waiting for the low half beyond 40 us, did not come.
